# A gated recurrence and an FFT convolution on one core: the filter loaded in long rows and rotated by permutation products, its second DFT in float32r, and x2 evicted by two engines

## The chip, the core and the metric

The kernel runs on one core of a Trainium2 chip. The core has a matrix engine (TensorE, PE in the profile; its weight loads are listed as PEld), a vector engine (VectorE, DVE), a scalar engine (ScalarE, ACT), GpSimd (POOL) and SyncE (SP), which here issues all transfers between device memory and on-chip memory. Each engine works through its own queue of instructions in order and waits on semaphores for the others. The metric is the device time of one execution in microseconds; three executions of the kernel before took 932.47, 933.0 and 933.32 us (median 933.0).

## The reference

Four sequences (B = 4) of S = 6272 steps and D = 256 channels. A gated recurrence runs over the steps, and its output goes through a gated long convolution whose filter is as long as the sequence.

```python
sig = 1.0 / (1.0 + np.exp(-f_logit))
f = lower_bound + (1.0 - lower_bound) * sig
for t in range(S):
    h = f[:, t] * h + (1.0 - f[:, t]) * x[:, t]
    y[:, t] = h
...
proj = y @ w_proj                      # 256 x 768
x1, x2, x3 = proj split in three
X2 = np.fft.rfft(x2, n=S, axis=1)
H = np.fft.rfft(filter_fft, n=S, axis=0)
x2_conv = np.fft.irfft(X2 * H, n=S, axis=1)
out = (x1 * x2_conv * x3) @ w_out      # 256 x 256
```

## The kernel before

The Fourier transform of length 6272 = 128 x 49 is done by matrix products, in a prime-factor form: one DFT of length 128 and one of length 49 whose two channels are packed into 98 rows. Channels are taken in 128 pairs (NEP), eight pairs (UE) to a unit, so sixteen units (NU).

The program has a prologue and then, for each of the four batches, the same passes:

- hgrn(b) is the recurrence, in 13 chunks of 512 steps (the last has 128). For a chunk SP loads x (tile xt) and f_logit (tile ft); ACT makes the sigmoid (sr, L140), POOL the product with x (ur, L142); PE transposes both in 128 x 128 blocks into PSUM banks 6 and 7 (L148, L150); ACT makes the gate (fT, L152), and DVE's scan (L155) writes the recurrence's output into HA, a float16 tile that holds both channel halves.
- wraps() copies pieces of HA inside on-chip memory, so that strided rows can run past the end of the sequence.
- prepare(tmp) is the filter and the constants: DFT matrices from iota and Sin, the projection weights scaled and split into a float16 value and a float16 residue, and then the filter. Its rows are loaded in 97 pieces (L308, L312): row number 128q + 49m of the sequence, modulo S, goes to partition m, so each of the 49 values of q needs a strided load of 1 KB rows that begins anew where the index wraps. The pieces lie in four slots (raws) inside a part of HA that is not yet in use. ACT casts them to float16 (f2h, L319), DVE subtracts to get the residue (f2l, L320), seven q at a time in four parts. Then each unit does the first DFT (24 products of 128 columns, L328 to L330), ACT writes the result as float16 (ah) and DVE its residue (al, L334) into the tile PP, and PE does the second DFT in 12 products of 512 columns (L345: value times value, residue times value, value times the residue of the matrix, FTl). ACT scales the result into H (L348).
- phase_p(b) makes x2 from HA and the weights (L380: 98 products of 256 columns in 13 rounds of at most four q), and ACT casts each round into x2 (L382). phase_f1(b) is the first DFT of x2 (L392), evicted by ACT and DVE in turn (L396, L398).
- units(b) does the second DFT, the product with H (L461), and the first step back (L469, L472); phase_z(b) makes x1 times x3 (L416 to L422). Both are woven with hgrn(b + 1). phase_o(b) finishes the inverse, multiplies, applies w_out and stores.

The order on every engine is set by a scheduler from the order in which the program is written. In the prologue weave() mixes the 13 chunks of hgrn(0) evenly with the steps of prepare: 2 steps of constants and weights, 7 of the filter's loading, 16 units and a last one. PSUM is one tile of 8 banks; pair() hands out its four pairs of banks in turn, also the pair 6 and 7.

Of the kernel before, what the change touches and what calls it, by code (L numbers as in the profile page):

```python
# [9 lines left out]
F32 = mybir.dt.float32  # L10
F16 = mybir.dt.float16
# [3 lines left out]
PSUM = bass.MemoryType.PSUM  # L15

# [3 lines left out]
S = 6272  # L20
# [19 lines left out]
def r_of(q):  # L40
    return (128 * q) % Q


def m0_of(q):
    return (128 * q) // Q


Q_OF_R = {r_of(q): q for q in range(Q)}


# [20 lines left out]
def kernel(  # L71
# [41 lines left out]

    raws = [HA[:, S + 3584 * k:S + 3584 * (k + 1)].bitcast(F32)
            .rearrange("m (q d) -> m q d", d=D) for k in range(4)]
# [13 lines left out]
    def hgrn(b):  # L129
        for c in range(NCHK):  # L130
            t0 = c * CH
            nb = min(CH, S - t0) // 128
            n = nb * 128
            xt = hg.tile([128, 4, D], F32, name="xt", tag="xt")
            nc.sync.dma_start(xt[:, 0:nb], x[b, t0:t0 + n, :].rearrange("(j p) d -> p j d", p=128))
            ft = hg.tile([128, 4, D], F32, name="ft", tag="ft")
            nc.sync.dma_start(ft[:, 0:nb], f_logit[b, t0:t0 + n, :]
                              .rearrange("(j p) d -> p j d", p=128))
            sr = hg.tile([128, 4, D], F32, name="sr", tag="sr")
            nc.scalar.activation(sr[:, 0:nb], ft[:, 0:nb], AF.Sigmoid, scale=-1.0)  # L140
            ur = hg.tile([128, 4, D], F32, name="ur", tag="ur")
            nc.gpsimd.tensor_tensor(ur[:, 0:nb], xt[:, 0:nb], sr[:, 0:nb], op=AOP.mult)  # L142
            for kh in range(2):
                cols = slice(kh * 128, kh * 128 + 128)
                sT = PS[:, 6, 0:n]
                uT = PS[:, 7, 0:n]
                for j in range(nb):
                    nc.tensor.transpose(sT[:, j * 128:(j + 1) * 128], sr[:, j, cols], iden[:])  # L148
                for j in range(nb):
                    nc.tensor.transpose(uT[:, j * 128:(j + 1) * 128], ur[:, j, cols], iden[:])  # L150
                fT = hg.tile([128, CH], F32, name="fT", tag="fT")
                nc.scalar.activation(fT[:, 0:n], sT, AF.Identity,  # L152
                                     scale=nomc[:, kh:kh + 1], bias=1.0)
                h0 = HB[kh] + t0
                nc.vector.tensor_tensor_scan(  # L155
                    HA[:, h0:h0 + n], fT[:, 0:n], uT,
                    0.0 if c == 0 else HA[:, h0 - 1:h0], op0=AOP.mult, op1=AOP.add)
            yield
# [8 lines left out]
    def prepare(tmp):  # L167
# [52 lines left out]
        c4 = icol([[4, 98]], 0, 0, 98, "c4")  # L220
        FTl = tmp.tile([128, 3, 128], F16, name="FTl")
        nc.vector.memset(FT[:], 0.0)
        nc.vector.memset(FTl[:], 0.0)
        for i, off in enumerate((49, 0, 98)):
# [8 lines left out]
            nc.vector.tensor_tensor(FTl[:98, i, 0:98], t[:98], FT[:98, i, 0:98],  # L233
                                    op=AOP.subtract)

        q4 = icol([[0, 2], [4, Q], [0, 2]], 0, 0, 196, "q4")
# [60 lines left out]

        f2h = cv.tile([128, NEP * TB + 32], F16, name="f2h", tag="x2")
# [3 lines left out]
        vh = f2h[:, 0:NEP * TB].rearrange("m (g p e q) -> m p e g q", p=2, e=2, q=Q)  # L302
        vl = f2l[:, 0:NEP * TB].rearrange("m (g p e q) -> m p e g q", p=2, e=2, q=Q)
        for q0 in range(0, Q, 7):
            raw = raws[(q0 // 7 + 2) % 4]
            for q in range(q0, q0 + 7):
                mm = -((128 * q - S) // Q)
                nc.sync.dma_start(raw[0:mm, q - q0, :],  # L308
                                  moe_filter_fft[128 * q:128 * q + Q * (mm - 1) + 1:Q, :])
                if mm < 128:  # L310
                    s0 = 128 * q + Q * mm - S
                    nc.sync.dma_start(raw[mm:128, q - q0, :],  # L312
                                      moe_filter_fft[s0:s0 + Q * (127 - mm) + 1:Q, :])
            for p in range(2):
                for e in range(2):
                    c0 = p * 128 + e * 64
                    src = raw[:, :, c0:c0 + 64].rearrange("m q g -> m g q")
                    dh, dl = vh[:, p, e, :, q0:q0 + 7], vl[:, p, e, :, q0:q0 + 7]
                    nc.scalar.copy(dh, src)  # L319
                    nc.vector.tensor_tensor(dl, src, dh, op=AOP.subtract)  # L320
            yield
        mX = tmp.tile([128, 2, 2, NEP], F16, name="mX")
        for u in range(NU):
# [7 lines left out]
            ah, al = PP[:, u % 2, 0], PP[:, u % 2, 1]  # L331
            pa4 = pa.rearrange("p i (r k) -> p r i k", r=2)
            nc.scalar.copy(ah[:TB], pa4[:TB])
            nc.vector.tensor_tensor(al[:TB], pa4[:TB], ah[:TB], op=AOP.subtract)  # L334
            for i, t in enumerate((ah, al)):
                nc.gpsimd.tensor_copy(
                    mX[:TB, i, :, u * UE:(u + 1) * UE],
                    t[:TB, :, :, 0])
            px = pair()
            for o, terms in ((0, ((0, 0), (1, 1))), (1, ((2, 0), (0, 1)))):  # L340
                seq = [(FT, ah), (FT, al), (FTl, ah)]
                n = 0
                for tb, r in terms:
                    for w, a in seq:
                        nc.tensor.matmul(px[:, o, :], w[:TB, tb, :], a[:TB, r, :, :],  # L345
                                         start=(n == 0), stop=(n == 5))
                        n += 1
# [4 lines left out]
        for o, tb in ((0, 0), (1, 2)):  # L352
            n = 0
            for w, i in ((FT, 0), (FT, 1), (FTl, 0)):
                nc.tensor.matmul(px[:, o, :, :], w[:TB, tb, :], mX[:TB, i, :, :],
                                 start=(n == 0), stop=(n == 2))
                n += 1
# [11 lines left out]
    def phase_p(b):  # L369
# [3 lines left out]
        xv = x2[:, 0:NEP * TB].rearrange("m (e q) -> m e q", q=Q)  # L373
        for q0 in range(0, Q, 4):
            qn = min(4, Q - q0)
            pp = pair().rearrange("m a (q e) -> m (a q) e", e=256)
            for q in range(q0, q0 + qn):
                for kh in range(2):
                    n0 = HB[kh] + 128 * q - (S if kh and q else 0)
                    nc.tensor.matmul(pp[:, q - q0, :], HA[:, n0:n0 + Q * 127 + 1:Q],  # L380
                                     W2[:, kh, :], start=(kh == 0), stop=(kh == 1))
            nc.scalar.copy(xv[:, :, q0:q0 + qn],  # L382
                           pp[:, 0:qn, :].rearrange("m q e -> m e q"))
            yield
# [91 lines left out]
    def phase_o(b):  # L476
        Th, z = st["Th"], st["z"]
        tf = Th[:].rearrange("p c g -> p (c g)")
        for r0 in range(0, Q, 4):
            rn = min(4, Q - r0)  # L480
            pc = pair()
            for i in range(rn):
                q = Q_OF_R[r0 + i]
                sh = (128 - m0_of(q)) % 128
                for rr in range(2):
                    c0 = (rr * Q + q) * 128
# [23 lines left out]
    with tc.tile_pool(name="tmp", bufs=1) as tmp:  # L510
        weave((hgrn(0), NCHK), (prepare(tmp), 2 + 7 + NU + 1))
# [52 lines left out]
```

## Time and profile before

| | value |
|---|---|
| runs | 932.47, 933.0, 933.32 us, median 933.0 |
| profiled execution | 931.49 us; its span 929.8 us, so 1.7 us lie outside the span |
| PE busy | 716.7 us (77%) |
| DVE busy | 533.9 us (57%) |
| ACT busy | 434.7 us (47%) |
| POOL busy | 145.4 us (16%) |
| mean granted TensorE clock | 0.982 |
| bytes moved | 98.00 MB, mean 105 GB/s |

How to read it: busy times overlap, so no share alone says what bounds the kernel. The page gives the busy share of each engine in 40 slices of the span (23.2 us each), the rate of transfers in the same slices, groups of instructions by line (busy time, mean time of one, and the idle time before them with what ended it), and the chain of work that ended last, followed back from the last instruction. The timeline lists single instructions. In a group's name the tile before the arrow is written and those behind it are read.

### The profile page before, as it was taken

How to read it: one execution, taken by the hardware profiler on the slowest of the kernel's cores; microseconds unless marked ns; L12 is line 12 of the kernel's file. 1: busy time of each engine (PE TensorE's matmuls, PEld its weight loads, DVE VectorE, ACT ScalarE, POOL GpSimd, SP SyncE). 2: the span in 40 equal slices, each digit the busy share in tenths (PEclk: the TensorE clock that was granted, in tenths of full speed). 3: DMA queues.
4: the chain of work that ended last, by engine and by line, in shares of the span. 5: the costliest groups of instructions: out<-in, count | busy, mean ns of one | idle time of the engine just before them, and what ended most of it. 6: DMA issues, size and time to landing. Idle time of an engine off the chain costs nothing.

```text
span 929.8 us, 14546 instructions
## 1 busy us (share of the span) xinstructions
PE 716.7 (77%) x5958; PEld 499.3 (54%) x5958; DVE 533.9 (57%) x585; ACT 434.7 (47%) x541; POOL 145.4 (16%) x173
## 2 busy tenths in 40 slices
PE   1110078997799998887999978789998887999877
PEld 1110055655555555775555557665565666655465
DVE  5833244441577777416777774177777640866753
ACT  2533155556644544376444533854444338433223
POOL 2211032222013323000133320002323000000000
PEclk9999999999899999998999999999999899999999
DMA  6133273324014347420153374202433241000024
GB/s 187 60 93 106 82 220 116 103 95 134 1 46 144 120 133 229 186 113 1 47 159 122 122 244 182 98 1 82 144 116 101 83 191 74 1 1 1 1 92 187
DMA packets 70699, 98.00 MB, mean 105 GB/s; under 512 B 3946, under 2 KB 61162, under 8 KB 70634
## 3 DMA queue, kind: packets, MB, share of 16 engines
q1 hardware_dynamic: 70634, 97.09, 31.2%
q8 instruction: 46, 0.75, 0.4%
q14 instruction: 19, 0.16, 0.1%
HBM read 58.85 MB, written 25.69 MB: 91 GB/s over the span
## 4 chain that ended last, share of the span: by engine, by line
PE 39%; DVE 26%; issue 13%; ACT 9%; DMA 7%; SPq 3%; POOL 2%; DVEq 0%; ACTq 0%; POOLq 0%
PE PS L469 9%; PE PS L416 9%; PE PS L501 7%; DVE z L422 7%; DVE PP L461 7%; DMA HA<-in_moe_filter_fft_dram 6%; ACT x L382 5%; DVE HA L155 5%; PE PS L345 3%; PE PS L150 3%; DVE z L493 2%; PE PS L148 2%; PE PS L392 2%; POOL ur L142 2%; SPq L312 1%
## 5 line engine op out<-in xcount | busy, mean ns | idle before, releaser
L416 PE MATMUL PS<-HA,W13h 128*128 128x490 f16 (+1 forms) x416 | 152.3, 366 | 15.0 <-DVE z L422 14.8
L416 PE MATMUL PS<-HA,W13l 128*128 128x490 f16 (+1 forms) x416 | 152.3, 366 | 0.0
L155 DVE TENSOR_TENSOR_SCAN HA<-fT,HA,PS 128x512 f16<-128x512 f32 (+1 forms) x96 | 116.1, 1209 | 62.3 <-PE PS L150 42.9
L461 DVE TENSOR_TENSOR PP<-PS,H 98x1008 f16<-98x1008 f32 x128 | 149.1, 1197 | 1.7 <-PE PS L457 1.7
L422 DVE TENSOR_TENSOR z<-PS,x1s 128x490 f16<-128x490 f32 (+1 forms) x104 | 101.0, 971 | 69.5 <-PE PS L416 58.5
L142 POOL TENSOR_TENSOR ur<-xt,sr 128x1024 f32<-128x1024 f32 (+1 forms) x52 | 116.7, 2245 | 132.3 <-ACT sr L140 111.6
L152 ACT ACTIVATE fT<-PS,nomc 128x512 f32<-128x512 f32 (+1 forms) x104 | 68.9, 662 | 136.7 <-PE PS L148 132.7
L148 PE MATMUL PS<-iden,sr 128*128 128x128 f32 x392 | 65.7, 289 | 69.1 <-ACT sr L140 66.9
L469 PEld LDWEIGHTS <-PP 98*128 98x128 f16 x1024 | 82.8, 97 | 65.9 <-DVE PP L461 39.6
L493 DVE TENSOR_TENSOR z<-PS,z 128x1024 f16<-128x1024 f32 (+1 forms) x52 | 58.2, 1159 | 90.0 <-PE PS L489 90.0
L501 PE MATMUL PS<-Woh,z 128*128 128x256 f16 x392 | 89.9, 278 | 20.8 <-DVE z L493 20.8
L454 POOL COPY PP<-zm 98x16 f16<-98x16 f16 x64 | 15.9, 256 | 542.8 <-PE PS L469 286.4
L469 PE MATMUL PS<-VB,PP 98*128 98x196 f16 x512 | 95.6, 248 | 4.6 <-DVE PP L461 4.5
L421 ACT ACTIVATE x1s<-PS 128x490 f32<-128x490 f32 (+1 forms) x104 | 60.0, 577 | 79.9 <-PE PS L416 79.7
L501 PEld LDWEIGHTS <-z 128*128 128x128 f16 x784 | 75.8, 100 | 34.9 <-DVE z L493 25.3
L505 ACT ACTIVATE osb<-PS 128x1024 f32<-128x1024 f32 (+1 forms) x52 | 50.7, 974 | 93.4 <-PE PS L501 89.5
L148 PEld LDWEIGHTS PS<-iden,sr 128*128 128x128 f32 x392 | 49.3, 149 | 82.2 <-ACT sr L140 60.1
L501 PE MATMUL PS<-Wol,z 128*128 128x256 f16 x392 | 89.5, 277 | 0.0
L396 DVE CAST HA<-PS 98x1024 f16<-98x1024 f32 x32 | 37.5, 1220 | 82.1 <-issue 57.5
L472 ACT CAST Th<-PS 128x784 f16<-128x784 f32 x64 | 51.7, 808 | 64.1 <-PE PS L469 64.1
L150 PE MATMUL PS<-iden,ur 128*128 128x128 f32 x392 | 67.0, 293 | 16.5 <-DVE HA L155 10.5
L469 PE MATMUL PS<-VA,PP 98*128 98x196 f16 x256 | 58.7, 248 | 19.9 <-DVE PP L461 17.1
(120 smaller groups left out, 1024.2 us busy)
## 6 DMA issues: line engine op xcount, KB each, us to landing
xt<-in_x_dram SPq DMA_DIRECT2D x48, 512.0 KB
ft<-in_f_logit_dram SPq DMA_DIRECT2D x48, 512.0 KB
out_dram<-osb SPq DMA_DIRECT2D x48, 512.0 KB
HA<-HA SPq DMA_DIRECT2D x12, 512.0 KB
HA<-HA SPq DMA_DIRECT2D x4, 544.0 KB
HA<-HA SPq DMA_DIRECT2D x4, 500.0 KB
HA<-HA SPq DMA_DIRECT2D x4, 480.0 KB
HA<-in_moe_w_proj_dram SPq DMA_DIRECT2D x1, 768.0 KB
```

What stands on the lines that cost most here:

```text
L142: nc.gpsimd.tensor_tensor(ur[:, 0:nb], xt[:, 0:nb], sr[:, 0:nb], op=AOP.mult)
L148: nc.tensor.transpose(sT[:, j * 128:(j + 1) * 128], sr[:, j, cols], iden[:])
L150: nc.tensor.transpose(uT[:, j * 128:(j + 1) * 128], ur[:, j, cols], iden[:])
L152: nc.scalar.activation(fT[:, 0:n], sT, AF.Identity, scale=nomc[:, kh:kh + 1], bias=1.0)
L155: nc.vector.tensor_tensor_scan(HA[:, h0:h0 + n], fT[:, 0:n], uT, 0.0 if c == 0 else HA[:, h0 - 1:h0], op0=AOP.mult, op1=AOP.add)
L416: nc.tensor.matmul(PS[:, 4 + i, 0:cn], w[:, kh, js], HA[:, h0:h0 + cn], start=(n == 0), stop=(n == 3))
L421: nc.scalar.activation(x1s[:, 0:cn], PS[:, 4, 0:cn], AF.Copy, scale=ZS)
L422: nc.vector.tensor_tensor(z[:, jb, :, m0:m0 + mn], PS[:, 5, 0:cn].rearrange("p (m r) -> p r m", r=Q), x1s[:, 0:cn].rearrange("p (m r) -> p ...
L461: nc.vector.tensor_tensor(P[:TB, o, :, :, 1:64], px.unsqueeze(1).broadcast_to([TB, 2, UE, 63]), hh, op=AOP.mult)
L469: nc.tensor.matmul(o, P[:TB, a, h, 2 * pr:2 * pr + 2, :], v[:TB], start=(n == 0), stop=(n == 3))
L493: nc.vector.tensor_tensor(zz, pc[:, :, 0:rn * 128].rearrange("p a (i m) -> p a i m", m=128), zz, op=AOP.mult)
L501: nc.tensor.matmul(po[:, i, :], z[:, kh, r0 + i, :], w[:, kh, :], start=(n == 0), stop=(n == 3))
```

## The change

It has five parts.

1. The filter is loaded in natural order: seen as 128 rows of 49 x 256 values, partition a gets rows 49a to 49a + 48, and seven loads fetch up to eight r at a time (8 KB in a row for each partition). Slots in raws grow from 3584 to 4096 columns. What the strided loads did is now done by PE: for each r a float32 product with a 128 x 128 slice of two identity matrices side by side (tile rot) rotates the 128 partitions by m0_of(r). ACT casts and DVE subtracts out of PSUM, four r at a time, in 13 rounds.
2. The 49 residues are kept in natural r order everywhere, and the DFT matrices' steps go from 4 to 72 (modulo 196) for it.
3. The filter's second DFT takes its first stage as one float32r tile (af), evicted by ACT and DVE in turn, and its matrix as one float32r tile FTr of 98 columns: 4 products of 512 columns in place of 12. The tile PP is not used in the prologue any more.
4. The sigmoid and the product with x are written over ft and xt, which get three buffers; sr and ur go.
5. phase_p's casts alternate between ACT and DVE.

weave() in the prologue now mixes the 13 chunks with 2 + 13 + 16 + 1 steps.

```diff
+def q_of(r):
+    return (18 * r) % Q
+def m0_of(r):
+    return (128 * q_of(r) - r) // Q
...
-    raws = [HA[:, S + 3584 * k:S + 3584 * (k + 1)].bitcast(F32)
+    raws = [HA[:, S + 4096 * k:S + 4096 * (k + 1)].bitcast(F32)
...
-            nc.scalar.activation(sr[:, 0:nb], ft[:, 0:nb], AF.Sigmoid, scale=-1.0)
-            nc.gpsimd.tensor_tensor(ur[:, 0:nb], xt[:, 0:nb], sr[:, 0:nb], op=AOP.mult)
+            nc.scalar.activation(ft[:, 0:nb], ft[:, 0:nb], AF.Sigmoid, scale=-1.0)
+            nc.gpsimd.tensor_tensor(xt[:, 0:nb], xt[:, 0:nb], ft[:, 0:nb], op=AOP.mult)
...
-        for q0 in range(0, Q, 7):
-            raw = raws[(q0 // 7 + 2) % 4]
-            for q in range(q0, q0 + 7):
-                mm = -((128 * q - S) // Q)
-                nc.sync.dma_start(raw[0:mm, q - q0, :],
-                                  moe_filter_fft[128 * q:128 * q + Q * (mm - 1) + 1:Q, :])
...
-            for p in range(2):
-                for e in range(2):
...
-                    nc.scalar.copy(dh, src)
-                    nc.vector.tensor_tensor(dl, src, dh, op=AOP.subtract)
+        ff = moe_filter_fft.rearrange("(a r) d -> a r d", r=Q)
+        for r0 in range(0, Q, 4):
+            rn = min(4, Q - r0)
+            raw = raws[(r0 // 8 + 2) % 4]
+            if r0 % 8 == 0:
+                rl = min(8, Q - r0)
+                nc.sync.dma_start(raw[:, 0:rl], ff[:, r0:r0 + rl, :])
+            pr = pair().rearrange("m a (r e) -> m (a r) e", e=256)
+            for r in range(r0, r0 + rn):
+                nc.tensor.matmul(pr[:, r - r0, :], rot[:, m0_of(r):m0_of(r) + 128],
+                                 raw[:, r % 8, :], start=True, stop=True)
+            src = pr[:, 0:rn, :].rearrange("m r (c g) -> m c g r", c=4)
+            dh, dl = vh[:, :, :, r0:r0 + rn], vl[:, :, :, r0:r0 + rn]
+            nc.scalar.copy(dh, src)
+            nc.vector.tensor_tensor(dl, src, dh, op=AOP.subtract)
...
-            nc.scalar.copy(ah[:TB], pa4[:TB])
-            nc.vector.tensor_tensor(al[:TB], pa4[:TB], ah[:TB], op=AOP.subtract)
+            if u % 2:
+                nc.scalar.copy(af[:TB], pa4[:TB])
+            else:
+                nc.vector.tensor_copy(af[:TB], pa4[:TB])
...
-                seq = [(FT, ah), (FT, al), (FTl, ah)]
...
+                for n, (tb, r) in enumerate(terms):
+                    nc.tensor.matmul(px[:TB, o, :], FTr[:TB, tb, :], af[:TB, r],
+                                     start=(n == 0), stop=(n == 1))
...
-            nc.scalar.copy(xv[:, :, q0:q0 + qn],
-                           pp[:, 0:qn, :].rearrange("m q e -> m e q"))
+            if i % 2:
+                nc.vector.tensor_copy(xv[:, :, r0:r0 + rn], src)
+            else:
+                nc.scalar.copy(xv[:, :, r0:r0 + rn], src)
```

Where instructions stand. First SP's queue at the start of the prologue, before: after the weights (L278, L280) come the filter's pieces, given as partitions by columns.

```order
L308 DMA HA<-in_moe_filter_fft_dram 128x256
L308 DMA HA<-in_moe_filter_fft_dram 126x256
L312 DMA HA<-in_moe_filter_fft_dram 2x256
L308 DMA HA<-in_moe_filter_fft_dram 123x256
L312 DMA HA<-in_moe_filter_fft_dram 5x256
L308 DMA HA<-in_moe_filter_fft_dram 121x256
```

The same queue now, from the weights on (L274, L276; the filter is L309):

```order
L274 DMA HA<-in_moe_w_proj_dram 128x2x768
L276 DMA HA<-in_moe_w_out_dram 128x2x256
L135 DMA xt<-in_x_dram 128x4x256
L137 DMA ft<-in_f_logit_dram 128x4x256
L309 DMA HA<-in_moe_filter_fft_dram 128x2048
L135 DMA xt<-in_x_dram 128x4x256
L137 DMA ft<-in_f_logit_dram 128x4x256
L309 DMA HA<-in_moe_filter_fft_dram 128x2048 x2
L135 DMA xt<-in_x_dram 128x4x256
L137 DMA ft<-in_f_logit_dram 128x4x256
```

Before, 13 pieces stood between the loads of chunk 0 and chunk 1, and 28 between later chunks; now one or two whole loads of the filter stand between chunks, and the weights are first.

Then DVE's queue around phase_p of batch 0, before (L334 is the residue of a unit, L371 a memset of x2's tail, L396 the eviction in phase_f1):

```order
L155 SCALAR_TENSOR_TENSOR HA<-fT,HA,PS 128x512 x2
L371 MEMSET x_1496 128x16
L334 TENSOR_TENSOR PP<-PS,PP 98x1024
L155 SCALAR_TENSOR_TENSOR HA<-fT,HA,PS 128x128 x2
L396 CAST HA<-PS 98x1024 x8
```

and now (L333 is DVE's share of the units' evictions, L373 its share of x2, L388 the eviction in phase_f1):

```order
L333 CAST af<-PS 98x1024
L153 SCALAR_TENSOR_TENSOR HA<-fT,HA,PS 128x512
L360 MEMSET x_1253 128x16
L153 SCALAR_TENSOR_TENSOR HA<-fT,HA,PS 128x128 x2
L373 CAST x_1253<-PS 128x256x4 x6
L388 CAST HA<-PS 98x1024 x8
```

Six casts of x2 have come between the last scan and phase_f1; ACT's queue keeps seven of its thirteen.

87 lines of the change are left out of this document (32 added, 55 removed).

## The prediction

> **What bounds the kernel now.** I read the slices of the span first, then the chain that ended last, then the busy times of the stretches that the chain marks off, then the rows of the instructions that the change touches. The span falls into a prologue (constants, filter, batch 0's recurrence), which ends at 222 us with the first product of phase_p, and four batch passes of some 184 us. The transfer rate by slices (each 23.2 us) is the first sign:
>
> ```profile
> GB/s 187 60 93 106 82 220 116 103 95 134 1 46 144 120 133 229 186 113 1 47 159 122 122 244 182 98 1 82 144 116 101 83 191 74 1 1 1 1 92 187
> ```
>
> Slices 2 to 5 move 60 to 106 GB/s, although other slices reach 220 to 244. The stretches (span, busy time of PE, PE's weight loads, DVE, ACT, POOL, granted clock, share of the transfer engines, GB/s):
>
> ```profile
> 0.00:20.00 20.00, 4.17 (x16) 3.00 (x16) 12.21 (x52) 5.40 (x6) 5.55 (x14) 1.00 0.58 183
> 20.00:120.00 100.00, 12.87 (x48) 8.87 (x48) 43.36 (x83) 36.57 (x45) 10.61 (x14) 1.00 0.33 99
> 120.00:222.00 102.00, 88.55 (x724) 58.33 (x724) 43.78 (x39) 56.14 (x72) 30.52 (x44) 1.00 0.41 130
> 222.00:240.00 18.00, 12.24 (x90) 10.74 (x91) 0.00 (x0) 16.68 (x13) 0.49 (x1) 0.81 0.17 57
> 255.00:368.00 113.00, 101.42 (x697) 65.35 (x697) 88.40 (x84) 52.59 (x78) 32.69 (x29) 1.00 0.40 127
> 405.00:423.00 18.00, 11.92 (x100) 10.78 (x98) 0.00 (x0) 16.98 (x15) 0.00 (x0) 0.94 0.12 46
> ```
>
> Three limits show. From 20 to 120 us no engine is busy half the time. From 120 to 222 us PE is busy 87%: the filter's two DFTs and the recurrence's transposes. In 222 to 240 us, and again in 405 to 423 us, ACT is busy 93 to 94% and DVE does nothing. The chain in order of time (start, us, what) says the same:
>
> ```profile
> 65.82 10.87 DMA HA<-in_moe_filter_fft_dram
> ...
> 98.88 11.30 DMA HA<-in_moe_filter_fft_dram
> ...
> 113.28 6.04 DMA xt<-in_x_dram
> ...
> 219.02 3.35 DMA HA<-HA
> ...
> 224.38 15.43 ACT x L382 x12
> ...
> 284.68 1.13 DVE PP L461
> 293.23 1.13 DVE PP L461
> ...
> 407.31 15.29 ACT x L382 x12
> ```
>
> Filter transfers that each lie 11 us on the chain, while the share of the transfer engines is a third: the 97 small pieces are the limit, not the bytes. SP's queue shows the back pressure; most pieces issue in about 0.3 us, but some take
>
> ```profile
> 94.47 4.37 SPq L308 DMA_DIRECT2D HA<-in_moe_filter_fft_dram  x1
> ...
> 99.51 4.88 SPq L308 DMA_DIRECT2D HA<-in_moe_filter_fft_dram  x1
> ```
>
> and x and f_logit of the next chunk stand behind them in the same queue.
>
> **1. Loading and splitting the filter (first DFT product now at 120.2 us).** Rows of the work that stays, goes or has a near relative (busy, mean ns | idle before), then PE's first DFT product and four transposes in the starved part:
>
> ```profile
> L320 DVE TENSOR_TENSOR f2l<-HA,f2h 128x448 f16<-128x448 f32 x28 | 25.1, 930 | 40.1 <-ACT f2h L319 21.1 <-DMA xt<-in_x_dram 10.2 <-DMA HA<-in_moe_filter_fft_dram 8.7
> L319 ACT CAST f2h<-HA 128x448 f16<-128x448 f32 x28 | 24.9, 960 | 49.8 <-DMA ft<-in_f_logit_dram 25.3 <-DMA HA<-in_moe_filter_fft_dram 24.5
> L155 DVE TENSOR_TENSOR_SCAN HA<-fT,HA,PS 128x512 f16<-128x512 f32 x88 | 112.3, 1276 | 58.1 <-PE PS L150 42.4 <-ACT fT L152 14.5 <-ACT sr L140 1.2
> L334 DVE TENSOR_TENSOR PP<-PS,PP 98x1024 f16<-98x1024 f32 x16 | 19.6, 1224 | 26.4 <-ACT PP L333 26.4
> L382 ACT CAST x<-PS 128x1024 f16<-128x1024 f32 x48 | 62.4, 1498 | 4.9 <-PE PS L380 4.9
> L382 ACT CAST x<-PS 128x256 f16<-128x256 f32 x4 | 6.1, 1514 | 0.0
> ```
>
> ```profile
> 58.12 1.11 PE L148 MATMUL PS<-iden,sr 128*128 128x128 f32 x4 [20.49 <-ACT sr L140]
> ...
> 120.20 0.39 PE L328 MATMUL PS<-D,f2h 128*128 128x128 f16 x2 [24.70 <-ACT f2h L319]
> ```
>
> The 97 pieces become 7 loads, six of 1 MB. By lanes, up to the last f2l write:
> - Transfers: weights 1.0, filter 6.4 and the six chunks that the new order issues ahead of the last filter load, 6.3: 13.7 MB. At 183 GB/s (the first stretch, weights and chunk rows) 75 us, at the best slice's 244 GB/s 56 us.
> - DVE: 55.6 us busy up to 120 us; without f2l (25.1, nearly all of it inside) some 32 us of constants and scans. Add 13 f2l of 1024 elements at 1.22 us (L334: two sources, one in PSUM) up to 2.1 us (L320's 2.1 ns an element, strided), 16 to 27 us, and four more scans, 5 us: 53 to 64 us.
> - ACT: 42.0 - 24.9 + 13 x 1.5 (L382 has the same short strided runs) + about 8 us for chunks and table loads = 45 us.
> - PE: 49 rotations of 256 float32 columns, new, with no such row; bounds under part 2. At twice float16's 0.107 us per 256 columns (part 3) 10 us, on PE's half speed 21 us, beside about 25 groups of four transposes at 0.6 to 1.1 us: 25 to 49 us.
>
> The lanes wait on each other in fixed order (PE to ACT to DVE inside each of 13 rounds, Sin tables in between), so I take 78 us: the slowest lane's upper bound plus the start. Bounds 62 (transfers at 244 GB/s, plus the start) and 95 us. Gain 120 - 78 = 42 us. What is late next is DVE with f2l.
>
> The Trainium skill ("FP8 and Floating Point Precision", TensorE Precision Notes) says that true float32 takes four passes through the array; by it a rotation would cost 4 x 0.107 = 0.43 us, an estimate, 21 us for all, still beside other lanes. No row here shows a float32 product that isn't a transpose.
>
> **2. The sixteen units of the filter's DFTs.** Timeline rows of DVE (the same row of two periods) and of PE:
>
> ```profile
> 144.73 1.23 DVE L334 TENSOR_TENSOR PP<-PS,PP 98x1024 f16<-98x1024 f32 x1 [2.32 <-ACT PP L333]
> ...
> 156.04 1.23 DVE L334 TENSOR_TENSOR PP<-PS,PP 98x1024 f16<-98x1024 f32 x1 [2.68 <-ACT PP L333]
> ```
>
> ```profile
> 153.34 0.22 PE L328 MATMUL PS<-D,f2h 128*128 128x128 f16 x1
> 153.40 0.22 PE L329 MATMUL PS<-D,f2l 128*128 128x128 f16 x1
> ...
> 158.83 0.59 PE L345 MATMUL PS<-PP,FT 98*128 98x512 f16 x2
> 159.26 0.38 PE L345 MATMUL PS<-PP,FTl 98*128 98x512 f16 x1
> 159.47 0.60 PE L148 MATMUL PS<-iden,sr 128*128 128x128 f32 x4
> 159.91 0.60 PE L150 MATMUL PS<-iden,ur 128*128 128x128 f32 x4
> ```
>
> Two units and one chunk take 11.3 us. From the starts, a product of 512 columns paces at 0.215 us (0.43 for two), one of 128 at 0.056. Two units are 24 x 0.215 + 48 x 0.056 = 5.2 + 2.7 us; a chunk is the rest, 3.4 us, its stalls included. The whole stage by this: 16 x 3.93 + 8.25 chunks x 3.4 = 91 us; measured 120.2 to 222.4, so 11 us of start and tail (the last chunk, its wrap copy of 3.35 us).
>
> After: 4 products of 512 in place of 12, and by the new order some 6.5 chunks left for this stage. A unit is 4 x 0.215 + 24 x 0.056 = 2.2 us; 16 x 2.2 + 6.5 x 3.4 = 57 us, plus the same 11: 68 us, 34 us less (28 from products, 6 from chunks that moved into part 1). The float32r product has no row. Lower bound: float16's 0.215. Upper: four float32 transposes pace at 0.44 (159.47 to 159.91), 0.11 each, twice a float16 product of as many columns, so 0.43: 64 x 0.215 = 14 us more. I take the lower, since a pass of 512 columns hides a weight load that one of 128 doesn't. The residue's subtract (L334, 19.6 us of DVE) goes, and a unit's eviction is one instruction on ACT or DVE: with chunks ACT has 2.5 us and DVE 1.6 us a unit, under PE's 3.6. The PSUM pair that units share with the recurrence (banks 6 and 7) stays shared.
>
> A rule that speaks against this: the Trainium skill ("TensorE: Matmul & The Clock Gate", Weight-path perf modes) gives the fast weight load only to 128 columns that aren't float32; FTr has 98, of float32r. By its P/1.2 the load is 82 ns, an estimate; if nothing hid it, 64 of them would add 5 us. The trace's float32 loads agree that they are slow (149 ns mean at L148 against 97).
>
> **3. phase_p, four times.** Now 13 casts on ACT set it, 15.4 us for twelve, 1.28 each, 17.4 us from 222.4 to 239.8; PE waits in each round:
>
> ```profile
> 232.32 1.03 PE L380 MATMUL PS<-W,HA 128*128 128x256 f16 x8 [0.26 <-ACT x L382]
> ```
>
> ```profile
> L396 DVE CAST HA<-PS 98x1024 f16<-98x1024 f32 x32 | 37.5, 1220 | 82.1 <-issue 57.5 <-PE PS L392 24.3
> L380 PE MATMUL PS<-W,HA 128*128 128x256 f16 x392 | 50.2, 279 | 8.0 <-ACT x L382 5.2 <-DMA HA<-HA 2.7
> ```
>
> A round's eight products pace at (1.03 - 0.28) / 7 = 0.107 us, 98 are 10.5 us. With ACT on seven rounds (9.0 us) and DVE on six, PE sets the pace: 10.5, a last cast of 1.5, and in the first batch 1.5 of cold start: 12.5 to 13.5 us. DVE's cast has no row in this layout; L396 (plain) gives 1.22, L320's rate 2.1 us, 7 to 13 us for six, so even the worst ties with PE. I take 4.5 us less each time, 18 us in all; bounds 12 and 20 from DVE's two ends. If PE fell to half speed throughout, 98 x 0.213 + 1.5 = 22.4 us, 5 us more each time: the upper end of this cost. PEclk of 0.94 in the second pass, at 66% busy, speaks against it.
>
> **4. The recurrence's tiles in place, three buffers.** Costed at nothing. In the batch passes the steps are 8.55 us apart (284.68 to 293.23) with PE at 90%, and the products and scans are the same. A buffer is now held until PE has transposed it, about 8 us (a step), then reloaded in 6 us (113.28), out of 3 x 8.55 = 25.6 us: 11 us of slack cover it. The order of r instead of q changes addresses only.
>
> Sum on the profiled execution's span: 929.8 - 42 - 34 - 18 = 835.8; with the 1.7 us outside the span, 837.5; that execution is 1.5 us under the median, so 839 us.
>
> **The rivals.**
> - Float32r runs like plain float32: between the transposes' factor of two, 839 + 14 = 853, and four passes, 0.86 each, 839 + 64 x 0.645 = 880. For it: every four-byte row here is at least twice as slow. Against: 512 columns, not 128. By the page named in part 1 four passes belong to true float32, and reduced precision reads the same words truncated.
> - The load stretch stays long: the rotations on PE at half speed (1.11 us for four transposes at 58 us, against 0.60 later), inside rounds that PE, ACT and DVE pass on one by one, 13 x about 7 us instead of 4. It would end at 105 to 115 us: 866 to 876.
> - phase_p doesn't gain, because both casts are bound by one write path (ACT's 1.51 us for 256 elements as for 1024 shows a cost per strided run) or PE clocks down: 857 to 877.
> - Slower: the in-place buffers starve the recurrence. If every one of the 39 chunks of batches 1 to 3 waited a whole load, 6.0 us, the time would be 839 + 235 = 1074; it is slower than before from 94 / 39 = 2.4 us a chunk. Against it the 11 us of slack.
> - Better: loads at 244 GB/s and rounds that pipeline, filter done by 62 us, and 20 us from phase_p: 821 or less.
>
> **How the numbers follow.** Forecast with its own bounds (815 to 856) 0.66; float32r slow 0.11; long load stretch 0.09; phase_p without gain 0.07; better than 815 0.05; starved recurrence 0.02. The range of 810 to 874 takes in the likely halves of the first three rivals. A change under 0.2% (1.9 us) can't be told from none in this kernel; only offsetting rivals would give it, 0.01, and slower 0.02.
>
> **What would show it.** Right: first L325 product near 78 us and transfers above 150 GB/s before it; L338 rows paced at 0.215 us, units 3.6 us apart with chunks; 13 phase_p casts split 7 and 6 with f1 starting about 13 us after the first product; steps of 8.55 us unchanged. Wrong: PE gaps before L312, an L338 pace of 0.43 or more, DVE casts over 2.1 us, waits of SP for PE in the batch passes.

## The result and the profile after

The changed kernel takes 833.0 us (median of four runs, 831.7 to 836.9) against 932.7 us for the kernel before beside it: a ratio of 0.894, with a 95% interval of 0.891 to 0.898. A second timing gave 830.2 against 931.1 us, 0.892 (0.890 to 0.894). The profiled execution took 831.66 us, its span is 830.0 us.

The rate of transfers in 40 slices, now of 20.75 us each:

```profile
GB/s 327 248 117 175 152 65 203 2 1 103 154 125 152 179 216 160 1 51 118 160 130 116 251 204 58 1 102 155 124 153 85 155 162 1 1 1 1 1 121 191
```

The starved slices at the start are gone. The busy times of the three stretches of the prologue that answer to those shown of before (span, PE, weight loads, DVE, ACT, POOL, granted clock, share of the transfer engines, GB/s), up to the first product of the filter's first DFT, from there to phase_p's steady products, and phase_p itself:

```profile
0.00:72.00 72.00, 39.98 (x179) 30.11 (x180) 57.37 (x125) 46.13 (x48) 24.10 (x33) 0.93 0.69 235
72.00:146.00 74.00, 59.71 (x576) 46.98 (x576) 29.59 (x26) 42.17 (x56) 20.55 (x25) 0.94 0.42 133
146.00:159.30 13.30, 11.72 (x88) 10.58 (x88) 8.51 (x6) 9.86 (x7) 1.14 (x1) 0.85 0.00 1
```

The first stretch is 48 us shorter and moves 235 GB/s where the starved one moved 99; DVE is busy in 80% of it. The second is 28 us shorter. In the third DVE, which had done nothing, works beside ACT. The new instructions by groups (busy, mean ns of one, idle time before them and what ended it), then the first DFT product and a run of second-DFT products from PE's timeline:

```profile
L312 PE MATMUL PS<-HA,rot 128*128 128x256 f32 x98 | 28.2, 433 | 4.9 <-DVE HA L153 3.9 <-DVE f2l L317 0.9
L317 DVE TENSOR_TENSOR f2l<-PS,f2h 128x1024 f16<-128x1024 f32 (+1 forms) x13 | 19.9, 1533 | 5.4 <-ACT f2h L316 5.4
L338 PE MATMUL PS<-af,FTr 98*98 98x512 f32 x64 | 19.1, 415 | 5.3 <-ACT af L331 2.2 <-DVE af L333 1.7 <-DVE HA L153 1.3
L338 PEld LDWEIGHTS PS<-af,FTr 98*98 98x98 f32 x64 | 9.1, 164 | 8.9 <-ACT af L331 2.8 <-issue 2.1 <-DVE HA L153 1.8
L373 DVE CAST x<-PS 128x1024 f16<-128x1024 f32 x24 | 34.5, 1444 | 20.2 <-PE PS L369 20.2
L375 ACT CAST x<-PS 128x1024 f16<-128x1024 f32 (+1 forms) x28 | 39.5, 1434 | 11.3 <-PE PS L369 11.1
L384 PE MATMUL PS<-D,x 128*128 128x128 f16 x512 | 32.8, 219 | 7.4 <-ACT x L375 6.5
```

```profile
71.93 0.61 PE L325 MATMUL PS<-D,f2h 128*128 128x128 f16 x4 [1.57 <-ACT f2h L316]
...
80.90 1.14 PE L338 MATMUL PS<-af,FTr 98*98 98x512 f32 x4 [0.66 <-DVE af L333]
81.88 0.23 PE L325 MATMUL PS<-D,f2h 128*128 128x128 f16 x1
```

Four float32r products of 512 columns take 0.98 us from the first's start to the next line's, 0.245 us each. The chain that ended last shows the new end of the prologue and a wait in the batch passes that the kernel before didn't have (start, us, what):

```profile
133.76 1.28 DVE HA L153
...
140.34 0.49 DVE HA L153
140.85 5.12 DMA HA<-HA
146.01 10.64 PE PS L369 x78
...
188.80 3.90 DMA ft<-in_f_logit_dram
...
199.44 4.58 DMA xt<-in_x_dram
204.19 2.13 POOL xt L140
```

```profile
L139 ACT ACTIVATE ft<-ft 128x1024 f32<-128x1024 f32 (+1 forms) x52 | 52.7, 1014 | 63.0 <-DMA ft<-in_f_logit_dram 62.5
```

The prologue now ends with the last scan of the recurrence and its wrap copy. ACT stood idle 63 us in all before the sigmoid (62.5 of it for loads of f_logit; 4.7 us before the change), 50 us of it in the batch passes.

By starts in the timelines, the 99.8 us of span came from here:

| stretch | before | after | gain | forecast |
|---|---|---|---|---|
| start to first DFT product | 120.2 | 71.9 | 48.3 | 42 |
| from there to phase_p | 102.2 | 74.1 | 28.1 | 34 |
| phase_p to the first f1 product, four times | 17.4, 18.6, 18.6, 18.7 | 13.4, 13.2, 13.2, 13.2 | 20.4 | 18 |
| f1, four times | 9.8, 10.5, 9.5, 9.6 | 8.4 each | 5.6 | none |
| units with z and hgrn | 121.0, 121.2, 121.0, 92.6 | 123.7, 121.4, 123.2, 91.1 | -3.5 | 0 |
| phase_o and the end | 33.4, 32.8, 34.9, 37.8 | 32.8, 32.9, 32.8, 39.6 | 0.8 | 0 |

### The profile page after: what moved, and what is told of

It is laid out like the page before. It is cut to its first block, busy times and chain, and to the rows that moved or that the text cites. A ratio compares the mean times of both kernels' runs of the same rounds, so it can differ in the third digit from the quotient of the medians.

```text
span 830.0 us, 14314 instructions
## 1 busy us (share of the span) xinstructions
PE 697.1 (84%) x5924; PEld 498.0 (60%) x5924; DVE 554.7 (67%) x587; ACT 400.5 (48%) x498; POOL 141.3 (17%) x157
## 4 chain that ended last, share of the span: by engine, by line
PE 39%; DVE 23%; DMA 10%; issue 8%; ACT 5%; POOL 1%; DVEq 0%; ACTq 0%; SPq 0%; POOLq 0%
PE PS L493 11%; DVE PP L453 8%; PE PS L461 8%; DMA ft<-in_f_logit_dram 7%; PE PS L408 7%; DVE z L414 6%; PE PS L369 5%; DVE z L485 4%; DVE HA L153 4%; PE PS L481 2%; ACT x1s L413 2%; DMA xt<-in_x_dram 2%; PE PS L146 2%; PE PS L148 1%; PE PS L384 1%
## 5 line engine op out<-in xcount | busy, mean ns | idle before, releaser
L408 PE MATMUL PS<-HA,W13h 128*128 128x490 f16 (+1 forms) x416 | 152.3, 366 | 17.6 <-DVE z L414 17.4
L140 POOL TENSOR_TENSOR xt<-xt,ft 128x1024 f32<-128x1024 f32 (+1 forms) x52 | 116.4, 2238 | 204.0 <-DMA xt<-in_x_dram 115.7
L153 DVE TENSOR_TENSOR_SCAN HA<-fT,HA,PS 128x512 f16<-128x512 f32 (+1 forms) x96 | 116.0, 1208 | 50.2 <-PE PS L148 29.8
L139 ACT ACTIVATE ft<-ft 128x1024 f32<-128x1024 f32 (+1 forms) x52 | 52.7, 1014 | 63.0 <-DMA ft<-in_f_logit_dram 62.5
L146 PE MATMUL PS<-iden,ft 128*128 128x128 f32 x392 | 63.7, 281 | 18.1 <-ACT ft L139 11.4
L148 PE MATMUL PS<-iden,xt 128*128 128x128 f32 x392 | 65.3, 288 | 13.0 <-DVE HA L153 6.7
L408 PEld LDWEIGHTS <-W13l 128*128 128x128 f16 x416 | 40.5, 97 | 58.3 <-issue 29.1
```

The costliest lines, as they stand in the source:

```text
L140: nc.gpsimd.tensor_tensor(xt[:, 0:nb], xt[:, 0:nb], ft[:, 0:nb], op=AOP.mult)
L146: nc.tensor.transpose(sT[:, j * 128:(j + 1) * 128], ft[:, j, cols], iden[:])
L148: nc.tensor.transpose(uT[:, j * 128:(j + 1) * 128], xt[:, j, cols], iden[:])
L153: nc.vector.tensor_tensor_scan(HA[:, h0:h0 + n], fT[:, 0:n], uT, 0.0 if c == 0 else HA[:, h0 - 1:h0], op0=AOP.mult, op1=AOP.add)
L408: nc.tensor.matmul(PS[:, 4 + i, 0:cn], w[:, kh, js], HA[:, h0:h0 + cn], start=(n == 0), stop=(n == 3))
```

## The experiments

Each timed run stands beside runs of the kernel before on the same chip; ratios are to that. The changed kernel was run again with the first three variants, as their yardstick. The later variants ran on other chips; differences from that yardstick's 830.2 us are given for them too, and the kernel before took 930.8 to 932.4 us on the four chips.

> The changed kernel itself, unaltered, as the yardstick for the three kernels that run beside it: both theories expect 833 us, the median of its first timing (831.7 to 836.9).

Measured: 830.2 us (829.7 to 833.4), ratio 0.892 (0.890 to 0.894).

**Tiles of their own in the batch passes.**

```diff
-            nc.scalar.activation(ft[:, 0:nb], ft[:, 0:nb], AF.Sigmoid, scale=-1.0)
-            nc.gpsimd.tensor_tensor(xt[:, 0:nb], xt[:, 0:nb], ft[:, 0:nb], op=AOP.mult)
+            sr, ur = ft, xt
+            if b:
+                sr = hg.tile([128, 4, D], F32, name="sr", tag="sr")
+                ur = hg.tile([128, 4, D], F32, name="ur", tag="ur")
+            nc.scalar.activation(sr[:, 0:nb], ft[:, 0:nb], AF.Sigmoid, scale=-1.0)
+            nc.gpsimd.tensor_tensor(ur[:, 0:nb], xt[:, 0:nb], sr[:, 0:nb], op=AOP.mult)
```

> The changed kernel, but in the hgrn passes of batches 1 to 3 the sigmoid and the product write tiles of their own (sr, ur), and xt and ft have two buffers, as in the kernel before; batch 0 keeps the in-place tiles. Theory A (the in-place tiles cost time: SP may load the next ft only once the transposes have read the last sigmoid, so that the sigmoid stands directly behind its load in ACT's queue and holds what is behind it): the wait of ACT's sigmoid for the load of ft, 62.6 us in the changed kernel, falls to 10 us or less, the three stretches from the last f1 eviction to the first product of phase_o's return fall from 123.7, 121.4 and 123.2 us to about 121.1 each, and the median is 4 to 6 us below the changed kernel's beside it, about 828. Theory B (those stretches are longer for another reason, such as a clock or where the batch starts, and the wait of ACT is slack): within 1 us of it, 833.

Measured: 825.3 us (824.5 to 827.7), 0.887 (0.885 to 0.889), 4.9 us under the yardstick. The group of the sigmoids of batches 1 to 3 in this kernel:

```profile
L144 ACT ACTIVATE sr<-ft 128x1024 f32<-128x1024 f32 (+1 forms) x39 | 39.0, 1000 | 0.0
```

The wait is gone, and from the last f1 product to the last product with H the three stretches are 118.7, 117.7 and 118.1 us against 120.5, 118.8 and 120.5 in the yardstick: 5.3 us, as much as the medians differ. Theory A holds. The two profiled executions differ by 8.2 us; 2.0 of these lie ahead of the first f1 product, in the prologue. There the last wrap copy, of the same size, took

```profile
139.24 3.43 DMA HA<-HA
```

in place of 5.12 and 5.14 us in the two profiles of the changed kernel. While it ran, the transfers moved 195 GB/s here and 306 in the changed kernel's first profile, where loads of batch 1 had been issued just ahead of it.

**Four buffers, still in place.** `bufs=3` became `bufs=3 if b == 0 else 4` for xt and ft.

> The changed kernel with its in-place tiles, but four buffers each of xt and ft in batches 1 to 3. Theory A (in place, the load of a buffer is released by the last transposes of its old chunk and the sigmoid of the new chunk follows directly behind that load, however many buffers there are): the ratio to the kernel before stays at 0.891 to 0.893 and ACT's sigmoid still waits 40 us or more for loads. Theory B (three buffers are too few, and a fourth gives the load its time): the time falls by 4 to 6 us as with separate tiles, a ratio of 0.886 to 0.888, and that wait falls below 20 us.

Measured: 833.2 us (832.9 to 834.1), 0.894 (0.893 to 0.895). The group of all its sigmoids:

```profile
L140 ACT ACTIVATE ft<-ft 128x1024 f32<-128x1024 f32 (+1 forms) x52 | 53.1, 1022 | 59.5 <-DMA ft<-in_f_logit_dram 59.1
```

Four buffers gain nothing: the ratio lies at, or just above, theory A's 0.891 to 0.893, and the sigmoid waits as long as before. The cause is the place; more than four buffers were not tried. The timelines of the changed kernel show the mechanism, SP's first and then ACT's:

```profile
188.80 0.37 SPq L137 DMA_DIRECT2D ft<-in_f_logit_dram  x1
```

```profile
190.19 0.81 ACT L464 CAST Th<-PS 128x784 f16<-128x784 f32 x1 [0.27 <-PE PS L461]
192.72 1.06 ACT L139 ACTIVATE ft<-ft 128x1024 f32<-128x1024 f32 x1 [1.71 <-DMA ft<-in_f_logit_dram]
193.68 0.56 ACT L413 ACTIVATE x1s<-PS 128x490 f32<-128x490 f32 x1
```

SP issues the load at 188.80, when the last transposes of that buffer's old sigmoid are done; the load takes 3.9 us; the sigmoid stands next in ACT's queue and waits 1.71 us for it; the eviction x1s stands behind the sigmoid, and DVE's z behind x1s. With a tile of its own ft is free once the sigmoid has read it, so the load starts earlier.

**The wrap copies cut.** To the second kernel, in wraps(): `(4096, E0)` became `(4096, 5632), (5632, E0)`, and `(4096, S)` likewise.

> The kernel with the separate tiles of the second run, and the last wrap copy of each half cut in two at column 5632, so that only its last 512 to 640 columns wait for the last scan. Theory A (the recurrence is now what ends the prologue, and behind its last scan stands a wrap copy that takes 5.12 us in the changed kernel): from the last scan to the first product of phase_p falls from 5.7 us to 4 us or less, 1 to 3 us off the median of the second run. Theory B (a wrap copy's time is a fixed cost whatever its size, or phase_p waits for something else): no change against the second run, within 1 us.

Measured: 823.5 us (819.8 to 826.0), 0.884 (0.881 to 0.887). From the last scan's start to the steady products of phase_p it is 2.8 us (139.06 to 141.86), 4.0 in the second kernel (138.73 to 142.71), 5.7 in the changed one. By the profiles theory A holds with 1.2 us; the times differ by 1.8 us, and their intervals overlap, so that the gain in time isn't shown.

**One caster in phase_p.** `nc.scalar.copy` for all 13 rounds.

> The changed kernel with all 13 casts of x2 in each phase_p on ACT again; all else as changed. Theory A (phase_p was paced by one engine's casts, and alternating them made the whole gain): 13 casts of about 1.45 us make phase_p 18 to 19 us and more again, 4 x 5.2 = 21 us, and up to 5 us more if the pauses let TensorE's next products run slower: 853 to 859. Theory B (phase_p is shorter because of the loads or the clock around it): below 842.

Measured: 860.8 us (860.5 to 864.1), 0.924 (0.921 to 0.927), 30.6 us above the yardstick. Groups of ACT's casts and of the first-DFT products behind them:

```profile
L372 ACT CAST x<-PS 128x1024 f16<-128x1024 f32 (+1 forms) x52 | 67.2, 1493 | 4.7 <-PE PS L369 4.7
L381 PE MATMUL PS<-D,x 128*128 128x128 f16 x512 | 38.1, 245 | 19.8 <-ACT x L372 18.4 <-ACT HA L387 1.2
```

phase_p is 18.6 us again in the second batch, 5.4 us more, and f1 takes 9.6 to 10.6 us in place of 8.4: its products average 245 ns instead of 219. Both parts of theory A are there, and the time lies a little above its 853 to 859 us. Some 3 of the 30.6 us are left; by the two profiles 2.5 us of them lie in the four stretches of units, and why is open.

**The two casters alone, in the kernel before.**

```diff
-            nc.scalar.copy(xv[:, :, q0:q0 + qn],
-                           pp[:, 0:qn, :].rearrange("m q e -> m e q"))
+            src = pp[:, 0:qn, :].rearrange("m q e -> m e q")
+            if i % 2:
+                nc.vector.tensor_copy(xv[:, :, q0:q0 + qn], src)
+            else:
+                nc.scalar.copy(xv[:, :, q0:q0 + qn], src)
```

> The kernel before, with the one edit that the casts of x2 in each phase_p go to ACT and DVE in turn. Theory A (this part of the change is worth 30 us by itself, as much as its undoing cost: 21 us of phase_p, 6 us of first-DFT products that run faster behind it, and some in what follows): 900 to 904 us. Theory B (only phase_p gets shorter, by the 18 to 20 us forecast; the rest of the 30 us hangs on the other parts of the change): 912 to 915 us.

Measured: 909.3 us (905.3 to 910.6), 0.975 (0.972 to 0.977): 23 us, between the two theories.

```profile
L395 PE MATMUL PS<-D,x 128*128 128x128 f16 x512 | 32.8, 219 | 7.5 <-ACT x L386 6.5
```

phase_p is 13.2 us and f1 8.4 us from the second batch on, as in the changed kernel. So this part is worth 20 us in phase_p and 5 to 6 in f1 by itself, and the other parts aren't needed for it. The whole is less than this sum: the last batch's units took 2.3 us longer than in the kernel before, and the cause of that is open.

**The second DFT as it was.** Back came the float16 pair ah and al, FTl, and twelve products of 512 columns a unit.

> The changed kernel with the filter's second DFT the old way: the first DFT evicted as a float16 pair, by ACT and then DVE, and twelve products of 512 columns a unit in place of four. Theory A (the units are paced by TensorE's products): 16 x (12 x 0.215 - 4 x 0.245) = 26 us more, 855 to 861, with the stage from the first DFT product to phase_p at about 100 us instead of 74. Theory B (the chunks of the recurrence pace the stage now, as its last scans do at the end of it): the stage grows by less than 15 us, below 848.

Measured: 859.5 us (857.3 to 862.6), 0.922 (0.919 to 0.926), 29 us above the yardstick. From the first DFT product to the first f1 product it is 112.6 us (73.55 to 186.12); in the changed kernel 87.4 (71.93 to 159.36). The 25.1 us come close to the expected difference of products, 16 x (12 x 0.215 - 4 x 0.245) = 25.6. So PE paces the units, and theory B is out; the eviction in two steps came back with the products, and its share isn't separated.

**The strided pieces back, everything else as changed.**

```diff
+                for r in range(r0, min(r0 + 8, Q)):
+                    q = q_of(r)
+                    mm = -((128 * q - S) // Q)
+                    nc.sync.dma_start(raw[0:mm, r - r0, :],
+                                      moe_filter_fft[128 * q:128 * q + Q * (mm - 1) + 1:Q, :])
...
+            src = raw[:, r0 % 8:r0 % 8 + rn, :].rearrange("m r (c g) -> m c g r", c=4)
```

> The changed kernel with the filter loaded in natural r order in strided pieces of 1 KB rows, one or two loads for each r, and no rotation; the casts read the loaded rows. Theory A (many small descriptors, not bytes, made the load stretch long): the first product of the filter's first DFT starts at 105 to 125 us again, not 72, and the time is 866 to 886. Theory B (it was the order of the rows, or the casts into strided columns, and not the form of the loads): it starts below 85 us, and the time is below 846.

Measured: 894.0 us (892.4 to 894.5), 0.959 (0.956 to 0.962), 64 us above the yardstick. PE's first DFT product, the stretch from 60 us on, and ACT's waits up to 128 us (total, times, longest):

```profile
128.82 0.31 PE L324 MATMUL PS<-D,f2h 128*128 128x128 f16 x1
```

```profile
60.00:128.00 68.00, 14.66 (x57) 10.66 (x58) 23.35 (x15) 25.33 (x21) 9.42 (x4) 1.00 0.40 122
```

```profile
ACT f2h L315 <- DMA HA<-in_moe_filter_fft_dram: 55.9, 10, 9.9
```

The form of the loads is the cause: with pieces the rate falls to 122 GB/s, and ACT waits 56 us for them, although the rotation's 49 products are gone here. The stretch and the time both lie above theory A's 105 to 125 and 866 to 886 us.

**The multiply left out in batch 0.** POOL's product with x is skipped for the prologue's chunks.

> The changed kernel with the multiply x * sigmoid on POOL left out in batch 0 alone, so that the recurrence of that batch takes x itself; the other batches keep it. Theory A (a DVE instruction that works on SBUF alone is held while POOL's multiply of 2.35 us runs, as the rows of 1.6 to 2.4 us beside those of 0.2 to 0.4 us suggest): no DVE instruction on a 98x98 or 98x196 tile is over 0.6 us, DVE's busy time in the load stretch falls by 6 to 9 us, and the first DFT product comes 4 to 9 us earlier, 63 to 68 us. Theory B (those rows are long because of what they read or of loads in flight): the long rows stay, and the first product stays at 70 us or later.

Measured in a single execution: 829.4 us, span 827.7. The rows of the same instruction in the changed kernel and here (ns: least, median, most), and the first DFT product:

```profile
L187 DVE TENSOR_SCALAR tv<-c_f,prow_f x3: 272/272/2349, 14.2 to 22.5; 98x98 f32<-98x98 f32 x3
```

```profile
L188 DVE TENSOR_SCALAR tv<-c_f,prow_f x3: 271/273/273, 13.7 to 23.4; 98x98 f32<-98x98 f32 x3
...
67.07 0.40 PE L326 MATMUL PS<-D,f2h 128*128 128x128 f16 x2 [1.57 <-ACT f2h L317]
```

The long rows are gone, DVE is busy 50.2 us up to there instead of 57.4, and the product comes 4.9 us earlier than in the changed kernel's first profile (3.6 than in its second). Theory A holds for the rows and the stretch. The time of this one execution can't be told from the yardstick's 830.2 us.

**The constant tables later.** Three kernels on top of the cut wrap copies. In the first the tables VA, VB, VN and ID stand behind the wrap copies in the program's text:

> The kernel of the third run, and the tables VA, VB, VN and ID, which nothing reads before the first batch's products, are computed behind the last wrap copy and not ahead of the filter's casts. Theory A (DVE is the lane that sets the load stretch, 57 us busy in its 72 us): the first product of the filter's first DFT starts 8 to 12 us earlier, at 60 to 64 us, the first product of phase_p 6 to 10 us earlier than in the third run, less 1 to 4 us for what the tables then delay of phase_p's casts on DVE: 4 to 8 us below the third run, about 820. Theory B (the load stretch is set by the transfers of filter and inputs, 235 GB/s over it): the stretch stays at 70 us or more and the time is within 2 us of the third run or above it.

Measured: 820.9 us (819.3 to 825.5), 0.882 (0.880 to 0.885). It decides nothing: the scheduler left them where they were, as DVE's row shows,

```profile
34.40 2.04 DVE L195 SCALAR_TENSOR_TENSOR tv<-q_f,prow_f,vao_f 98x196 f32<-98x196 f32 x1
```

and the first product stayed at 70.8 us. In the second a data dependence holds them back, `in0=last, scalar=0.0` with an element of f2l:

> The kernel of e2_wrap_cut (separate tiles, cut wrap copies), with the tables VA, VB, VN and ID made to read an element of f2l times zero, so that they cannot be computed before the filter's casts; in e3_constants_late they had stood later in the program's text only, and ran at 34 to 70 us all the same. Theory A (DVE is the lane that sets the load stretch): 10 to 12 us of DVE's work leave it, the first DFT product starts 7 to 11 us earlier than 71.5 us, at 60 to 65, the tables fit into DVE's free time of the units stage (29 us busy of 66), and the time is 6 to 10 us below 823.5: 813 to 818. Theory B (the last loads of the filter, or the products that wait for a PSUM pair shared with the recurrence, set the end of the stretch): it ends at 69 us or later, and the time is within 2 us of 823.5. Theory C (the stretch is shorter, but the scans of the recurrence, which end the prologue, are held up by the tables): the first product comes 7 us earlier, and the time is still above 820.

Measured: 820.7 us (819.5 to 824.6), 0.881 (0.879 to 0.883); not to be told from the cut wrap copies' 0.884, and above theory A's 813 to 818 us. Products begin at 64.1 us, but only four of them; the others begin at 71.6 us, behind the residue of one more group of four r, which came behind part of the tables in DVE's order:

```profile
61.27 1.29 DVE L329 TENSOR_TENSOR f2l<-PS,f2h 128x256 f16<-128x256 f32 x1
62.17 2.12 DVE L259 SCALAR_TENSOR_TENSOR late<-f2l,prow_f 128x1 f32<-128x1 f16 x1
...
68.19 1.55 DVE L329 TENSOR_TENSOR f2l<-PS,f2h 128x1024 f16<-128x1024 f32 x1
```

In the third the rotations use PSUM pairs 0 to 2 only (`k3 = (r0 // 4) % 3`), and the tables follow every f2l:

> The kernel of e9_constants_tied, and two further edits: the rotations of the filter take PSUM pairs 0 to 2 in turn, not 0 to 3 (pair 3 is banks 6 and 7, which the recurrence's transposes use in every chunk), and the tables are tied to f2l's last column, so that all casts of the filter stand ahead of them on DVE. Theory A (in the changed kernel and in e9 the last group of rotations is the one that waits for the scans to free banks 6 and 7, and its cast ends the load stretch at 70 to 73 us): with no sharing the last f2l cast ends at 62 to 67 us, the steady run of first-DFT products begins there and not at 71.6 us, and the time is 4 to 8 us below e9's, 813 to 817, a ratio of 0.872 to 0.877. Theory B (the last loads, or the three pairs' own turn through two casts each, set the end): the last f2l cast ends at 69 us or later and the ratio is 0.879 to 0.883. Theory C (the stretch ends earlier, but the recurrence's chunks end the prologue and are no earlier): last f2l cast by 67 us, last scan at 136 us or later as in e9 (137.2), and a ratio above 0.878.

Measured: 828.4 us (819.1 to 829.9), 0.888 (0.885 to 0.892). The steady products do begin at 63.2 us, as theory A has it (two edits were made at once, so that neither is shown to do it alone), and nothing is won: the last scan starts at 142.5 us, against 136.7 in the kernel above. Theory C. Part of the loss may lie in the clock: the profiled execution took 829.5 us at a mean granted clock of 0.979, and one of the six took 819.1 us at 0.996. ACT's timeline shows one of the places where it went:

```profile
97.89 1.28 ACT L209 ACT_TABLE_LOAD   x1
99.18 0.51 ACT L209 ACTIVATE id<-tqf,pi_col 128x256 f32<-128x256 f32 x1
99.60 0.67 ACT L155 ACTIVATE fT<-PS,nomc 128x512 f32<-128x512 f32 x1
100.28 1.28 ACT L144 ACT_TABLE_LOAD   x1
103.28 1.06 ACT L144 ACTIVATE ft<-ft 128x1024 f32<-128x1024 f32 x1 [1.71 <-DMA ft<-in_f_logit_dram]
104.24 0.99 ACT L344 CAST af<-PS 98x1024 fp32r<-98x1024 f32 x1
```

The tables' Sin between two sigmoids costs two table loads of 1.28 us, the sigmoid waits for its in-place load, and the unit's eviction stands behind all of it. From the steady DFT products to the first f1 product it is 95.0 us (63.2 to 158.2) against 81.0 (71.6 to 152.5). How much of these 14 us each of the waits makes, and why PE's clock was 0.74 to 0.84 between 92 and 116 us, is open.

The kernel with tiles of its own and cut wrap copies beats both kernels (0.884; 0.882 and 0.881 with the tables later); of the edits behind it none adds what the measurement can tell, and the last one takes some away.

## Why the prediction was right

839 us were forecast and 833.0 measured, inside the range and inside the forecast's own bounds. The terms:

- **Load stretch: 42 forecast, 48.3 measured.** The cause was as named: the pieces put back brought the stretch to 128.8 us. Of the lanes, DVE with 57.4 us, ACT with 46.1 and PE with 40.0 came out as given; the term was too cautious where it took the transfers at the first stretch's 183 GB/s, for that stretch already held 17 of the pieces. They ran at 235 GB/s and brought 16.9 MB in the 72 us, more than the 13.7 counted. What ended the stretch was no lane's sum but an order: PE's last group of rotations uses PSUM banks 6 and 7 in turn with the recurrence's transposes, these waited for a scan, and the group then ran slowly, at a granted clock of 0.69 from 60 to 72 us:

```profile
65.79 1.12 PE L148 MATMUL PS<-iden,xt 128*128 128x128 f32 x4 [1.83 <-DVE HA L153]
66.70 3.65 PE L312 MATMUL PS<-HA,rot 128*128 128x256 f32 x8
```

  DVE's f2l, which was named as what is late next, then waited 3.68 us for ACT's cast and so for these products. PE's rotations, which had no row, cost as much as four float16 products: a run of eight records at full clock,

```profile
55.84 1.89 PE L325 MATMUL PS<-HA,rot 128*128 128x256 f32 x8
```

  from the kernel with three pairs, paces at (1.89 - 0.38) / 7 = 0.216 us, and a rotation is two records: 0.43 us. By the Trainium skill ("FP8 and Floating Point Precision", TensorE Precision Notes) true float32 takes four passes, an estimate of 0.43; the trace agrees.
- **Sixteen units: 34 forecast, 28.1 measured.** The mechanism was right (the second DFT undone costs 25.1 us there), the sizes were off in three places: a product paces at 0.245 us in a run of four (0.275 in runs of two), not 0.215, 64 x 0.03 = 1.9 us or a little more; the last wrap copy took 5.12 us, not 3.35, 1.8 us, and 3.43 again in the kernel with tiles of its own; and 16 of the 26 scans, 7.25 chunks, were left for this stage, not 6.5, 0.75 x 3.4 = 2.6 us. Together 6.3 us, where 6.1 were missing (74.1 against the sum's 68); so close a fit is in part chance. Two units are 7.6 us apart (79.56 to 132.65 in seven steps of L333), 3.8 each, where 3.6 was given. Float32r didn't run like float32, whose 512 columns were put at 0.43 or 0.86 us. The rule of the fast weight load ("TensorE: Matmul & The Clock Gate" in the Trainium skill, Weight-path perf modes) would have cost 5 us if nothing hid those loads; 98 columns of float32r do load slowly, 164 ns, twice the estimated 82 and more than the 97 of float16's 128 columns, but only some 2 us shows, and whether that is the load or the product itself isn't separated.
- **phase_p: 18 forecast, 20.4 measured**, 13.2 us each time as given; the difference is that phase_p had been 18.6 us in the last three batches, and the sum used the first's 17.4. DVE's cast is 1.44 us, near the lower end of 1.22 to 2.1. Not forecast at all were 5.6 us in f1: with no pauses for ACT in phase_p, its products run at 219 ns instead of 244. The granted clock of f1's first 5.5 us in batch 0 had been 0.67, and it is 1.00 now over the whole of that f1; the two casters alone, put into the kernel before, gave the 219 ns too.
- **In-place tiles: 0 forecast, 5 us measured.** This step failed. No scan starved (DVE stood idle 50.2 us before its scans, against 62.3 before the change), and 39 chunks lost some 0.13 us each, far from the 2.4 us of the rival. But the slack of 11 us was counted for the recurrence alone. The sigmoid needs the load at the place where it stands in ACT's queue, and what is held there is not the chunk but x1s and fT of other work behind it. The steps of 8.55 us in the middle of a pass became 8.64 to 9.28 (195.19 to 203.97 is 8.78). The prediction had named the sign of it, waits of SP for PE in the batch passes, and had costed it at nothing.

The errors of the first and second term, 6 us each and of opposite sign, cancelled, which is luck; the gain in f1 paid for the in-place tiles; phase_p's 2.4 us, 0.8 us in the last stretches and 1.5 us in the units of the last batch make up most of the 6 us between forecast and result.

## What to carry to other kernels

When the transfer engines are busy a third of the time and yet a stretch waits for them, look at the size of the pieces before the bytes, and let an idle matrix engine do the reordering that strided loads did. Cost a tile that is overwritten in place at the queue of the engine that writes it: count the free time from the last reader to that instruction's turn, and name what stands behind it. When one lane of a pipelined stretch is relieved, ask for the next wait in the same order of work: here 8 us less in the load stretch came back in full in the stage behind it, in part perhaps by a lower clock.

## What the runs showed of the hardware

DVE instructions whose operands all lie in on-chip SBUF (not in PSUM) were held until POOL's multiply ended. Rows of DVE, two long ones and a scan, and of POOL in the changed kernel:

```profile
14.21 2.35 DVE L187 TENSOR_SCALAR tv<-c_f,prow_f 98x98 f32<-98x98 f32 x1
...
47.24 1.69 DVE L196 CAST tqf<-tqi 128x256 f32<-128x256 int32 x1
48.86 1.27 DVE L153 TENSOR_TENSOR_SCAN HA<-fT,HA,PS 128x512 f16<-128x512 f32 x1
```

```profile
13.67 2.82 POOL L140 TENSOR_TENSOR xt<-xt,ft 128x1024 f32<-128x1024 f32 x1
...
46.41 2.37 POOL L140 TENSOR_TENSOR xt<-xt,ft 128x1024 f32<-128x1024 f32 x1 [2.47 <-ACT ft L139]
```

The first ends at 16.56 us where POOL's ends at 16.49, the second at 48.93 and 48.78; without the multiply they take 0.27 and 0.28 us. Scans and f2l, which read one operand from PSUM, keep their 1.27 and 1.53 us beside such a multiply. The Trainium skill ("SBUF — State Buffer", Who interferes with whom) tells of a port pair that DVE and GpSimd share under an exclusive lock; the trace agrees, and here it made 7 us of DVE's busy time look like work.
